# Four ordering edits in a four-layer linear-attention and gated-FFN kernel: products on zeros ahead of the work, the first K chunks slab by slab, a 16-bit exponential, and the FFN norm two steps later

## Chip, cores and metric

One core of a Trainium2 chip. The metric is the device time of one launch in microseconds (us).

## What is computed

`x` has 2048 rows of 1024 bf16 values. Layers A and B are applied in turn, twice, with the same weights:

```
x = x + A(layernorm(x));  x = x + B(layernorm(x));  x = x + A(layernorm(x));  x = x + B(layernorm(x))

A:  q, k, v = split(x @ wqkv) in 32 heads of 32;  phi(t) = (t+1 if t > 0 else exp(t)) + 1e-6
    kv = sum_s phi(k) v;  z = sum_s phi(k);  o = phi(q) kv / (phi(q) z + 1e-6);  out = o @ wo
B:  out = ((x @ w_gate) * (x @ w_up)) @ w_down          (1024 -> 3584 -> 1024)
```

## The kernel before

Rows lie in 16 tiles of 128 (`t`), four of which make a group of 512. The residual `X` stays in SBUF as bf16. Nothing is scheduled by a compiler: the program is the order in which the Python code emits instructions. Each engine takes its own in that order. Plans (`at(step, function, ...)`) say after which step of a loop a side job is emitted. Buffers come from first-in first-out lists: 16 `slots` of 1 MB, 13 `temps` of 128x512 f32, and 8 PSUM `banks`.

**Start.** SyncE (SP) issues the loads in a written order: X tiles 0 and 1, the first 512 columns of the K weights (a "slab", 1 MB, `load_cols`, L96), X tiles 2 and 3, the second K slab, X tile 4, the first V slab, and so on. Tiles 0 to 3 are normalised first. `ln_stats` (L158, L159) makes mean and variance on VectorE (DVE). `ln_norm` makes 1/sqrt on ScalarE (ACT; L166 is Ln, L168 is Exp) and the normalised tile `xn` on DVE (L170). For the first group of the first layer, `tr_tile` transposes `xn` by eight TensorE (PE) products with the identity (L187) into one bank, and ACT copies the bank to SBUF (L188). For all other groups the transpose is a DMA issued by SP (L182).

**Layer A, first loop.** A K or V chunk `kv_chunk(t, n)` is eight accumulating products of 128x128 by 128x512 (L369) of tile t with slab n (0 and 1 are K, 2 and 3 are V). It waits for its transposed tile and its slab. A group takes 16 chunks: first K for its four tiles, with slabs 0 and 1 alternating, then V. Each K chunk goes through `phi`: ACT takes exp of the bank into a temp (L193), DVE makes min(.,1)+1e-6 in the temp (L194), and DVE adds max(bank,0) to it (L195). The bank goes back only after L195. `kp` (L386) accumulates phi(k) times V. In the first layer weight statistics are taken beside it (squares on ACT L202, statistics on DVE L207).

**Layer A, second loop.** Step i of 44 emits: `den_step(i-4)` (a product L501; Ln and Exp on ACT, L503 and L506; a multiply on DVE, L509, which makes one of the eight pieces of a group's scaled phi(q)), `q_step(i)` (eight products L487, then `phi`), `out_step(i-12)` (eight products L517, one for each piece; DVE adds the bank to X, L519), then side jobs. The first `out_step` of a group, at steps 12, 20, 28 and 36, needs the eighth piece, whose L509 is emitted one step earlier. Side jobs of the first layer are maxima over weights on DVE (L222) and the weight scales. `ahead_of` plans the FFN's preparation in both A layers: for u = 0..7 statistics, norm and transpose of tile u at steps 18+2u, 19+2u and 20+2u; casts and sums of the first weights (`W.cast`, `W.sums`, L312 and L327); sums of the transposed rows (`t_sums`, L349 to L357) at steps 36 to 39.

**Layer B.** `ffn_pass` runs 14 `quad` steps of 56 products (L646) for each half of the rows, in a seven-product scheme for blocks of 2x2, and `down_seven` the way back (L868). The first quad reads the transposed rows, then `t_sums` 0, 1, 2 and 3 in that order. In the first B layer GpSimd (POOL) also casts `w_down` (`prep_load`, `prep_cast`, L571).

Of the kernel before, what the change touches and what calls it, by code (L numbers as in the profile page):

```python
# [9 lines left out]
ACT = mybir.ActivationFunctionType  # L10
ALU = mybir.AluOpType
AX = mybir.AxisListType
BF16 = mybir.dt.bfloat16
F16 = mybir.dt.float16
F32 = mybir.dt.float32
# [19 lines left out]
def kernel(  # L35
# [11 lines left out]
    nc = tc.nc  # L47
    P = 128
# [3 lines left out]
    KD = D // P  # L52
    KH = KD // 2
    KF = F // P
    G = 512
    NG = S // G
    TPG = G // P
    NB = 512
    DC = D // NB
# [7 lines left out]
    small = ctx.enter_context(tc.tile_pool(name="small", bufs=4))  # L67
# [6 lines left out]
    wqkv_v = A_wqkv.rearrange("(k p) n -> p k n", p=P)  # L74
# [7 lines left out]
    temps = Free([const.tile([P, NB], F32, tag=f"f{i}", name=f"f{i}") for i in range(13)])  # L82
    banks = Free([psum.tile([P, NB], F32, tag=f"b{i}", name=f"b{i}") for i in range(8)])

    def v3(s, n):
        return s[:].rearrange("p (k n) -> p k n", n=n)
# [4 lines left out]
    def load_x(t):  # L91
        nc.sync.dma_start(out=X[:, t, :], in_=x_view[:, t, :])

    def load_cols(view, n):
        s = slots.get()
        nc.sync.dma_start(out=v3(s, NB), in_=view[:, :, n * NB:(n + 1) * NB])  # L96
        return s

    nc.scalar.preload_act_table_set("natural_log_exp_and_others")
    wA = {}  # L100
    load_x(0)
    load_x(1)
    wA["k"] = [load_cols(wqkv_v, DC)]
    load_x(2)
    load_x(3)
    wA["k"].append(load_cols(wqkv_v, DC + 1))
    load_x(4)
    wA["v"] = [load_cols(wqkv_v, 2 * DC)]
    load_x(5)
    load_x(6)  # L110
    wA["v"].append(load_cols(wqkv_v, 2 * DC + 1))
    for t in range(7, NT):
        load_x(t)

    ident = const.tile([P, P], BF16, tag="ident", name="ident")
    make_identity(nc, ident[:])
    mask = const.tile([P, P], F32, tag="mask", name="mask")
# [30 lines left out]
    NST = D // FMAX  # L148
# [2 lines left out]
    xqs = {}  # L151
    lns = {}

    def ln_stats(li, t):
        mv = small.tile([P, 2], F32, tag="mv", name="mv")
        st = small.tile([P, NST, 6], F32, tag="st", name="st")
        for c in range(NST):
            nc.vector.bn_stats(out=st[:, c, :], in_=X[:, t, c * FMAX:(c + 1) * FMAX])  # L158
        nc.vector.bn_aggr(out=mv[:], in_=st[:])  # L159
        lns[(li, t)] = mv  # L160

    def ln_norm(li, t):
        mv = lns[(li, t)]
        half = li % 2 == 1
        rstd = small.tile([P, 1], F32, tag="rstd", name="rstd")
        nc.scalar.activation(out=rstd[:], in_=mv[:, 1:2], func=ACT.Ln, bias=(eps5x if half else eps5)[:],  # L166
                             scale=1.0 / (XS * XS) if half else 1.0)
        nc.scalar.activation(out=rstd[:], in_=rstd[:], func=ACT.Exp, scale=-0.5)  # L168
        xn = xnp.tile([P, D], F16 if half else BF16, tag="xn", name="xn")
        nc.vector.tensor_scalar(out=xn[:], in0=X[:, t, :], scalar1=mv[:, 0:1], scalar2=rstd[:],  # L170
                                op0=ALU.subtract, op1=ALU.mult)
        lns[(li, t)] = xn

    def tr_tile(li, t):
        xn = lns.pop((li, t))
        g, tl = divmod(t, TPG)
        if (li, g) not in xnTs:
            xnTs[(li, g)] = slots.get()
        s = xnTs[(li, g)]
        xnT = (h3 if li % 2 == 1 else v3)(s, NB)  # L180
        if (li, g) != (0, 0):
            nc.sync.dma_start_transpose(out=xnT[:, :, tl * P:(tl + 1) * P], in_=xn[:])  # L182
            return
        b = banks.get()
        pt = b[:].bitcast(BF16).rearrange("p (k n) -> p k n", n=P)
        for k in range(KD):
            nc.tensor.transpose(out=pt[:, k, :], in_=xn[:, k * P:(k + 1) * P], identity=ident[:])  # L187
        nc.scalar.copy(out=xnT[:, :, tl * P:(tl + 1) * P], in_=pt)  # L188
        banks.put(b)

    def phi(b, dst):
        m = temps.get()
        nc.scalar.activation(out=m[:], in_=b[:], func=ACT.Exp)  # L193
        nc.vector.tensor_scalar(out=m[:], in0=m[:], scalar1=1.0, scalar2=1e-6, op0=ALU.min, op1=ALU.add)  # L194
        nc.vector.scalar_tensor_tensor(out=dst, in0=b[:], scalar=0.0, in1=m[:], op0=ALU.max, op1=ALU.add)  # L195
        temps.put(m)

    def scan(i):
# [160 lines left out]
    def layer_A(li, ahead):  # L359
# [3 lines left out]
        def kv_chunk(t, n):  # L363
            g, tl = divmod(t, TPG)
            xnT = v3(xnTs[(li, g)], NB)
            w = v3(wA["k"][n] if n < DC else wA["v"][n - DC], NB)
            b = banks.get()
            for k in range(KD):
                nc.tensor.matmul(out=b[:], lhsT=xnT[:, k, tl * P:(tl + 1) * P], rhs=w[:, k, :],  # L369
                                 start=(k == 0), stop=(k == KD - 1))  # L370
            if n < DC:
                if g not in pks:
                    pks[g] = slots.get()
                phi(b, v3(pks[g], D)[:, tl, n * NB:(n + 1) * NB])
            else:
                c0 = (n - DC) * (NB // P)
                nc.scalar.copy(out=vbs[t % NV][:, c0:c0 + NB // P, 0:P],
                               in_=b[:].rearrange("p (c f) -> p c f", f=P))
            banks.put(b)
# [15 lines left out]
        def at(step, f, *args):  # L395
            plan.setdefault(step, []).append((f, args))

        NCH = 2 * DC * TPG
        for t in range(TPG, NT):
            i = (t // TPG - 1) * NCH + 3 * (t % TPG)  # L400
            at(i + 3, ln_stats, li, t)
            at(i + 5, ln_norm, li, t)
            at(i + 6, tr_tile, li, t)
        for t in range(NT - TPG):
            at((t // TPG + 1) * NCH + 3, kp, t)
        if li == 0:
            for t, i in ((1, 0), (2, 1), (3, 3)):
                at(i, tr_tile, li, t)
        at(2 * NCH + 4, lambda: wA.update(q=[load_cols(wqkv_v, n) for n in range(DC)]))
        at(3 * NCH + 4, lambda: wA.update(o=[load_cols(wo_v, n) for n in range(DC)]))  # L410
        if li == 0:
# [12 lines left out]
            for i, t0, t1 in ((10, 16, 24), (0, 16, 25), (1, 16, 28), (2, 20, 31), (3, 32, 36), (11, 32, 39),  # L424
# [3 lines left out]
                at(t1, spend, i, 0)  # L428
                at(t1 + 1, spend, i, 1)
        for i in range(NG * NCH):  # L430
            q, j = divmod(i, NCH)
            half, j = divmod(j, DC * TPG)
            tl, n = divmod(j, DC)
            kv_chunk(q * TPG + tl, half * DC + n)
            for f, args in plan.get(i, []):
                f(*args)
        slots.put(*wA.pop("k"), *wA.pop("v"))
# [43 lines left out]
        def q_step(g, c):  # L481
            xnT = v3(xnTs[(li, g)], NB)
            w = v3(wA["q"][c // (NB // P)], NB)
            j = c % (NB // P)
            b = banks.get()
            for k in range(KD):
                nc.tensor.matmul(out=b[:], lhsT=w[:, k, j * P:(j + 1) * P], rhs=xnT[:, k, :],  # L487
                                 start=(k == 0), stop=(k == KD - 1))
            pq[(g, c)] = temps.get()
            phi(b, pq[(g, c)][:].bitcast(BF16)[:, 0:G])  # L490
            banks.put(b)
            if c == KD - 1:
                slots.put(xnTs.pop((li, g)))
                if g == NG - 1:
                    slots.put(*wA.pop("q"))
# [279 lines left out]
    def down_seven(q, li, p, hs, wd, load_piece, cast_piece, ORDER, at, run, finish, xrow, nl, W2, load_a, final):  # L775
# [31 lines left out]
        if nl[0] < 4:  # L807
            for u in range(2 * TPG if p == 0 else TPG):
                t = nl[1] * 2 * TPG + u
                at(2 + 7 * u, ln_stats, nl[0], t)  # L810
                at(4 + 7 * u, ln_norm, nl[0], t)
                at(5 + 7 * u, tr_tile, nl[0], t)
# [81 lines left out]
    def ahead_of(li, W):  # L894
        plan = {}

        def at(step, *what):
            plan.setdefault(step, []).append(what)

        for u in range(2 * TPG):  # L900
            at(18 + 2 * u, ln_stats, li, u)
            at(19 + 2 * u, ln_norm, li, u)
            at(20 + 2 * u, tr_tile, li, u)
        at(22, W.load, 0)
        at(28, W.load, 1)
        for i in range(4):
            at(25 + i, W.cast, 0, i)
            at(34 + i, W.cast, 1, i)
            at(36 + i, t_sums, li, 0, i)
        at(35, W.sums, 0)  # L910
        at(41, W.sums, 1)
        if li == 1:
            at(36, prep_load, 0)
            at(38, prep_load, 1)
            at(40, prep_cast, 0)
        return plan

    for t in range(TPG):
        ln_stats(0, t)
        ln_norm(0, t)  # L920
        if t == 0:
            tr_tile(0, 0)
    for li in (0, 2):
        W = Weights(li)
        layer_A(li, ahead_of(li + 1, W))
        layer_B(li + 1, W)
# [30 lines left out]
```

## Time and profile before

| what | us |
|---|---|
| median of 3 runs | 1515.45 (1515.42 to 1516.24) |
| the profiled execution's own time | 1515.59 |
| span in the profile | 1513.8 |
| outside the span | 1.79 |
| PE busy | 1499.7 |
| DVE busy | 952.5 |
| ACT busy | 736.2 |
| POOL busy | 90.0 |

Times in the views count from the start of the span. A timeline row is: start, length, engine, line, operation, output and input tiles, number of merged instructions, and in brackets the engine's idle time before it with what ended it. Ends of products are modelled, so one row of products can overlap the next; starts are the sharper measure. DMA rows are issues on SP ("SPq"); the view of issues gives the time from the issue to the landing.

### The profile page before, as it was taken

How to read it: one execution, taken by the hardware profiler on the slowest of the kernel's cores; microseconds unless marked ns; L12 is line 12 of the kernel's file. 1: busy time of each engine (PE TensorE's matmuls, PEld its weight loads, DVE VectorE, ACT ScalarE, POOL GpSimd, SP SyncE). 2: the span in 40 equal slices, each digit the busy share in tenths (PEclk: the TensorE clock that was granted, in tenths of full speed). 3: DMA queues.
4: the chain of work that ended last, by engine and by line, in shares of the span. 5: the costliest groups of instructions: out<-in, count | busy, mean ns of one | idle time of the engine just before them, and what ended most of it. 6: DMA issues, size and time to landing. Idle time of an engine off the chain costs nothing.

```text
span 1513.8 us, 18314 instructions
## 1 busy us (share of the span) xinstructions
PE 1499.7 (99%) x7155; PEld 689.1 (46%) x7155; DVE 952.5 (63%) x1595; ACT 736.2 (49%) x1111; POOL 90.0 (6%) x46
## 2 busy tenths in 40 slices
PE   7999999999999999999999999999999999999999
PEld 3454444444444444444445444444444444444444
DVE  6567998988677566667355467854444853444452
ACT  4677875777535477762133365523334222333420
POOL 0000004963000000000000000000000000000000
PEclk9999999999999999999999999999999999999999
DMA  7696246475358788758413300563333678333523
GB/s 239 152 302 225 84 90 189 121 218 159 117 135 240 239 264 263 243 197 247 160 28 84 84 1 8 148 234 139 140 111 129 165 258 342 113 139 139 193 75 129
DMA packets 213399, 247.61 MB, mean 164 GB/s; under 512 B 68416, under 2 KB 189248, under 8 KB 202560
## 3 DMA queue, kind: packets, MB, share of 16 engines
q1 hardware_dynamic: 213312, 246.44, 51.6%
q8 instruction: 56, 0.92, 0.2%
q14 instruction: 31, 0.25, 0.0%
HBM read 189.79 MB, written 40.89 MB: 152 GB/s over the span
## 4 chain that ended last, share of the span: by engine, by line
PE 94%; DVE 4%; ACT 1%; DMA 1%; issue 0%; SPq 0%
PE b L646 45%; PE b L868 22%; PE b L369 12%; PE b L517 6%; PE b L487 6%; PE b L386 1%; DVE dmx L222 1%; PE b L501 1%; ACT s L202 1%; DVE wst L207 1%; DVE f L195 1%; DMA s<-in_A_wqkv_dram 1%; DVE f L194 1%; ACT f L193 0%; DVE s L195 0%; PE b L469 0%
## 5 line engine op out<-in xcount | busy, mean ns | idle before, releaser
L646 PE MATMUL b<-s,s 128*128 128x512 f16 x3136 | 677.5, 379 | 0.0
L646 PEld LDWEIGHTS <-s 128*128 128x128 f16 x3136 | 306.9, 98 | 370.0
L868 PE MATMUL b<-s,s 128*128 128x512 f16 x1568 | 339.1, 379 | 0.0
L662 DVE TENSOR_TENSOR f<-f,b 128x512 f32<-128x512 f32 x232 | 159.0, 686 | 229.1 <-ACT f L651 214.6
L651 ACT COPY f<-b 128x512 f32<-128x512 f32 x284 | 165.9, 584 | 228.0 <-PE b L646 228.0
L868 PEld LDWEIGHTS <-s 128*128 128x128 f16 x1568 | 153.4, 98 | 185.0
L369 PE MATMUL b<-s,s 128*128 128x512 bf16 x1024 | 225.0, 381 | 2.5 <-DMA s<-in_A_wqkv_dram 2.2
L369 PEld LDWEIGHTS <-s 128*128 128x128 bf16 x1024 | 100.3, 98 | 122.7 <-issue 3.9
L193 ACT ACTIVATE f<-b 128x512 f32<-128x512 f32 x128 | 75.5, 595 | 106.5 <-PE b L369 85.7
L613 ACT ACTIVATE s<-s,scw 128x1792 f16<-128x1792 bf16 x48 | 83.1, 1785 | 90.7 <-DMA s<-in_B_w_down_dram 52.7
L312 ACT ACTIVATE s<-s,scw 128x1024 f16<-128x1024 bf16 x112 | 122.9, 1152 | 3.3 <-DMA s<-in_B_w_gate_dram 2.1
L657 ACT COPY b<-b 128x512 f32<-128x512 f32 x104 | 59.2, 570 | 128.3 <-PE b L646 128.3
L517 PE MATMUL b<-s,s 128*128 128x512 bf16 x512 | 118.5, 379 | 1.9 <-DVE s L509 1.9
L487 PE MATMUL b<-s,s 128*128 128x512 bf16 x512 | 120.3, 379 | 0.0
L571 POOL TENSOR_SCALAR s<-s,scw 128x1024 f16<-128x1024 bf16 x28 | 88.3, 3170 | 263.4 <-DVE X L519 246.1
L194 DVE TENSOR_SCALAR f<-f 128x512 f32<-128x512 f32 x128 | 53.9, 421 | 75.2 <-ACT f L193 74.3
L665 DVE SCALAR_TENSOR_TENSOR s<-f,b 128x512 f16<-128x512 f32 x108 | 74.1, 686 | 40.9 <-PE b L646 24.5
L665 DVE SCALAR_TENSOR_TENSOR s<-f,f 128x512 f16<-128x512 f32 x116 | 82.5, 711 | 4.0
L158 DVE BATCH_NORM_STATS2 st<-X 128x6 f32<-128x512 bf16 x128 | 81.8, 680 | 4.4 <-DMA X<-in_A_x_dram 4.4
L517 PEld LDWEIGHTS <-s 128*128 128x128 bf16 x512 | 50.1, 98 | 62.6 <-DVE s L509 2.4
L487 PEld LDWEIGHTS <-s 128*128 128x128 bf16 x512 | 50.0, 98 | 59.6
L841 DVE SCALAR_TENSOR_TENSOR X<-b,kap,f 128x512 bf16<-128x512 f32 x48 | 32.7, 744 | 60.6 <-PE b L868 60.6
(80 smaller groups left out, 850.6 us busy)
## 6 DMA issues: line engine op xcount, KB each, us to landing
s<-wc SPq DMA_DIRECT2D x56, 1024.0 KB, 6.2
s<-dc SPq DMA_DIRECT2D x32, 896.0 KB, 6.3
wc<-s SPq DMA_DIRECT2D x28, 1024.0 KB, 4.9
s<-in_B_w_down_dram SPq DMA_DIRECT2D x24, 896.0 KB, 5.1
s<-in_B_w_down_dram SPq DMA_DIRECT2D x14, 1024.0 KB, 7.4
s<-in_B_w_gate_dram SPq DMA_DIRECT2D x28, 512.0 KB, 5.8
s<-in_B_w_up_dram SPq DMA_DIRECT2D x28, 512.0 KB, 6.8
s<-in_A_wqkv_dram SPq DMA_DIRECT2D x12, 1024.0 KB, 8.9
```

Source lines behind the costliest of these rows:

```text
L158: nc.vector.bn_stats(out=st[:, c, :], in_=X[:, t, c * FMAX:(c + 1) * FMAX])
L312: nc.scalar.activation(out=h, in_=v, func=ACT.Copy, scale=scw[:, m:m + 1])
L369: nc.tensor.matmul(out=b[:], lhsT=xnT[:, k, tl * P:(tl + 1) * P], rhs=w[:, k, :], start=(k == 0), stop=(k == KD - 1))
L487: nc.tensor.matmul(out=b[:], lhsT=w[:, k, j * P:(j + 1) * P], rhs=xnT[:, k, :], start=(k == 0), stop=(k == KD - 1))
L517: nc.tensor.matmul(out=b[:], lhsT=v3(pqs[g], G)[:, c, tl * P:(tl + 1) * P], rhs=v3(M[n], NB)[:, c, :], start=(c == 0), stop=(c == KD - 1))
L571: nc.gpsimd.tensor_scalar(out=h3(s, D)[:, i, :], in0=v3(s, D)[:, i, :], scalar1=scw[:, 2:3], scalar2=None, op0=ALU.mult)
L613: nc.scalar.activation(out=v.bitcast(F16)[:, r * w:(r + 1) * w], in_=v[:, r * w:(r + 1) * w], func=ACT.Copy, scale=scw[:, 2:3])
L646: nc.tensor.matmul(out=o[m][:], lhsT=W.get(j, m, st[i - 1], k), rhs=mv[i - 1][:, k, :], start=start and k == 0, stop=stop and k == KH - 1, ...
L651: nc.scalar.copy(out=d[m][:], in_=o[m][:])
L662: nc.vector.tensor_tensor(out=d[m][:], in0=d[m][:], in1=o[m][:], op=ALU.add)
L665: nc.vector.scalar_tensor_tensor(out=hv[:, 2 * (j % 2) + r, g * G:(g + 1) * G], in0=x[:], scalar=HS, in1=y[:], op0=ALU.mult, op1=ALU.mult)
L868: nc.tensor.matmul(out=bank[(key, tl)][:], lhsT=lhs(i, j, tl), rhs=h3(wd[2 * pi + j // WPC], NB)[:, j % WPC, :], start=(j == 0 and i in (1 ...
```

## The change

- One new helper, `warm_up(n)`, emits n products of 128x128 by 128x512 on a temp set to zero by DVE. Eleven are emitted ahead of everything else on PE, and four between tile 0's transposes and the first chunk.
- The first K slab is loaded by two DMAs of 512 KB (four of its eight row blocks each).
- The first four chunks run in the order (tile 0, slab 0), (1, 0), (0, 1), (1, 1) instead of (0, 0), (0, 1), (1, 0), (1, 1). The transposes of tiles 1, 2 and 3 are emitted inside chunks: tile 1's after the sixth product of the first chunk, tile 2's after the fourth of the third, tile 3's after the fourth of the fourth. `ln_norm` of tiles 2 and 3 and half of tile 3's statistics move into the chunks too.
- The copy out of a transpose's bank becomes two, four blocks each, and ACT's copies of tiles 0 and 1 stand ahead of the Ln and Exp of the next tile.
- `phi` writes its exponential as bf16 into the temp's first half, and both DVE instructions read it there.
- In both A layers, `ln_stats`, `ln_norm` and `tr_tile` of the FFN move from steps 18, 19, 20 + 2u to 20, 21, 22 + 2u, and `t_sums` from 36 to 39 to steps 39 to 42.

```diff
-    def load_cols(view, n):
+    def load_cols(view, n, parts=1):
         s = slots.get()
-        nc.sync.dma_start(out=v3(s, NB), in_=view[:, :, n * NB:(n + 1) * NB])
+        w = KD // parts
+        for r in range(parts):
+            nc.sync.dma_start(out=v3(s, NB)[:, r * w:(r + 1) * w, :],
+                              in_=view[:, r * w:(r + 1) * w, n * NB:(n + 1) * NB])
...
-    wA["k"] = [load_cols(wqkv_v, DC)]
+    wA["k"] = [load_cols(wqkv_v, DC, 2)]
...
+    warm = temps.get()
+    nc.vector.memset(warm[:], 0.0)
+    warmb = banks.get()
+
+    def warm_up(n):
+        for _ in range(n):
+            nc.tensor.matmul(out=warmb[:], lhsT=warm[:].bitcast(BF16)[:, 0:P], rhs=warm[:].bitcast(BF16)[:, 0:NB],
+                             start=True, stop=True)
+
+    warm_up(11)
...
-        nc.scalar.copy(out=xnT[:, :, tl * P:(tl + 1) * P], in_=pt)
+        nc.scalar.copy(out=xnT[:, 0:KH, tl * P:(tl + 1) * P], in_=pt[:, 0:KH])
+        nc.scalar.copy(out=xnT[:, KH:KD, tl * P:(tl + 1) * P], in_=pt[:, KH:KD])
...
-        nc.scalar.activation(out=m[:], in_=b[:], func=ACT.Exp)
-        nc.vector.tensor_scalar(out=m[:], in0=m[:], scalar1=1.0, scalar2=1e-6, op0=ALU.min, op1=ALU.add)
-        nc.vector.scalar_tensor_tensor(out=dst, in0=b[:], scalar=0.0, in1=m[:], op0=ALU.max, op1=ALU.add)
+        e = m[:].bitcast(BF16)[:, 0:NB]
+        nc.scalar.activation(out=e, in_=b[:], func=ACT.Exp)
+        nc.vector.tensor_scalar(out=e, in0=e, scalar1=1.0, scalar2=1e-6, op0=ALU.min, op1=ALU.add)
+        nc.vector.scalar_tensor_tensor(out=dst, in0=b[:], scalar=0.0, in1=e, op0=ALU.max, op1=ALU.add)
...
             for k in range(KD):
                 nc.tensor.matmul(out=b[:], lhsT=xnT[:, k, tl * P:(tl + 1) * P], rhs=w[:, k, :],
                                  start=(k == 0), stop=(k == KD - 1))
+                for f, *args in mid.get((t, n, k), ()):
+                    f(*args)
...
         if li == 0:
-            for t, i in ((1, 0), (2, 1), (3, 3)):
-                at(i, tr_tile, li, t)
+            order[0:4] = [(0, 0), (1, 0), (0, 1), (1, 1)]
+            mid.update({(0, 0, 5): ((tr_tile, 0, 1), (ln_norm, 0, 2), (ln_stats, 0, 3, (1,))),
+                        (1, 0, 5): ((ln_norm, 0, 3),),
+                        (0, 1, 3): ((tr_tile, 0, 2),), (1, 1, 3): ((tr_tile, 0, 3),)})
...
         for u in range(2 * TPG):
-            at(18 + 2 * u, ln_stats, li, u)
-            at(19 + 2 * u, ln_norm, li, u)
-            at(20 + 2 * u, tr_tile, li, u)
+            at(20 + 2 * u, ln_stats, li, u)
+            at(21 + 2 * u, ln_norm, li, u)
+            at(22 + 2 * u, tr_tile, li, u)
...
-            at(36 + i, t_sums, li, 0, i)
+            at(39 + i, t_sums, li, 0, i)
...
-    for t in range(TPG):
-        ln_stats(0, t)
-        ln_norm(0, t)
-        if t == 0:
-            tr_tile(0, 0)
+    ln_stats(0, 0)
+    ln_stats(0, 1, (0,))
+    ln_norm(0, 0)
+    tr_tile(0, 0)
+    ln_stats(0, 1, (1,))
+    ln_norm(0, 1)
+    ln_stats(0, 2)
+    ln_stats(0, 3, (0,))
+    warm_up(4)
+    temps.put(warm)
+    banks.put(warmb)
```

## The prediction

> **What bounds the kernel now.** First the page's busy row and its costliest groups, then the waits of PE, then the timelines of PE and DVE where those waits stand.
>
> ```profile
> PE 1499.7 (99%) x7155; PEld 689.1 (46%) x7155; DVE 952.5 (63%) x1595; ACT 736.2 (49%) x1111; POOL 90.0 (6%) x46
> ...
> L194 DVE TENSOR_SCALAR f<-f 128x512 f32<-128x512 f32 x128 | 53.9, 421 | 75.2 <-ACT f L193 74.3
> ```
>
> PE is busy 1499.7 of 1513.8 us: only PE's idle time and slow products can be won, and work on other engines counts only where PE waits for it. The second row is phi's middle instruction on DVE, 421 ns. The waits of PE, with the total, the count and the longest in us:
>
> ```profile
> PE b L187 <- DVE xn L170: 6.4, 1, 6.4
> PE b L369 <- DMA s<-in_A_wqkv_dram: 2.2, 1, 2.2
> PE b L517 <- DVE s L509: 1.9, 1, 1.9
> PE b L369 <- DVE s L195: 0.2, 1, 0.2
> ```
>
> Four waits in the whole run; the change touches all. Now the start of PE's timeline:
>
> ```profile
> 6.36 1.04 PE L187 MATMUL b<-ident,xn 128*128 128x128 bf16 x8 [6.36 <-DVE xn L170]
> 9.62 3.57 PE L369 MATMUL b<-s,s 128*128 128x512 bf16 x8 [2.22 <-DMA s<-in_A_wqkv_dram]
> 12.98 1.06 PE L187 MATMUL b<-ident,xn 128*128 128x128 bf16 x8
> 14.04 2.29 PE L369 MATMUL b<-s,s 128*128 128x512 bf16 x8
> 16.17 0.61 PE L187 MATMUL b<-ident,xn 128*128 128x128 bf16 x8
> 16.62 3.62 PE L369 MATMUL b<-s,s 128*128 128x512 bf16 x16
> 20.07 0.61 PE L187 MATMUL b<-ident,xn 128*128 128x128 bf16 x8
> 20.52 0.81 PE L369 MATMUL b<-s,s 128*128 128x512 bf16 x3
> ```
>
> Read starts against counts. The eight products from 9.62 take 3.36 us to the next row, 427 ns each after the first; from 16.62 sixteen take 3.45, 216 ns each. The weight loads, 0.43 us apart up to 14.85 and then five in 0.99 us, date the change of clock to 14.9. (The granted-clock column prints 1.00 for these stretches too, so spacing is the only sign.) Work from 9.62 to 20.52 is 32 products and 24 transposes, at full speed 32 x 0.216 + 24 x 0.056 = 8.26 us, and took 10.90.
>
> The two K slabs' rows in the view of issues (KB, us to landing):
>
> ```profile
> s<-in_A_wqkv_dram SPq DMA_DIRECT2D x1, 1024.0 KB, 7.9
> ```
> ```profile
> s<-in_A_wqkv_dram SPq DMA_DIRECT2D x1, 1024.0 KB, 10.7
> ```
>
> Issued at 1.64 and 3.31, they land at 9.6 and 14.0. The first product starts at 9.62; the first one on slab 1 at 14.04, 0.2 us after the transposes before it would let it. So the start is bound by two landings, not by the clock alone. X tile 1, next ahead of slab 0, landed at 4.1.
>
> The one long wait behind the start, on PE and then on DVE:
>
> ```profile
> 189.82 1.67 PE L517 MATMUL b<-s,s 128*128 128x512 bf16 x7
> 193.42 0.39 PE L517 MATMUL b<-s,s 128*128 128x512 bf16 x1 [1.93 <-DVE s L509]
> ```
>
> ```profile
> 187.37 2.28 DVE L222 TENSOR_REDUCE dmx<-s 128x1 f32<-128x2048 bf16 x1
> 191.55 1.28 DVE L158 BATCH_NORM_STATS2 st<-X 128x6 f32<-128x512 bf16 x2
> 192.86 0.21 DVE L159 BATCH_NORM_AGGREGATE mv<-st 128x2 f32<-128x12 f32 x1
> 192.99 0.37 DVE L509 TENSOR_TENSOR s<-f,f 128x512 bf16<-128x512 bf16 x1
> ```
>
> PE could have started its eighth product at 189.82 + 7 x 0.216 = 191.33 and started it at 193.42: 2.09 us. It lacked the L509 at 192.99, and DVE was doing the statistics of u=0 (191.55 to 192.99, 1.44 us) ahead of it, with no gap since L194 at 161.2.
>
> **Start, term by term.** The memset on DVE is bounded by the nearest rows: 0.20 us (POOL's MEMSET of 128x128 f32) and 0.69 (the slowest DVE row of 128x512 f32). DVE is idle until 3.56, so it costs nothing; PE begins at 1.0 to 1.5. Eleven products at 427 ns take 4.7 us and end by 6.2, before `xn` 0 at 6.36, so they delay nothing. The extra statistics of tile 1 (half of the 1.28 us row) fill the 0.66 us in which DVE waited for ACT before L170. Transposes 6.36 to 6.8 (at 56 ns) or 7.2 (at 107, as before).
>
> When does the clock rise? Before, 5.3 us after the first product at 9.62. The same 5.3 from 1.5 gives 6.8. [...]
>
> The four further products end at 7.7 (or 8.9 with a cold clock). ACT's copy was 1.01 us for 1024 columns; a half is about the 0.59 us of the 128x512 bank cast (L377), so the first half is in SBUF at 7.6 and the second at 8.1. Half a slab should land at 4.1 + 5.5/2 = 6.8, the other at 9.6. So four products run from 7.7, the fifth waits for 9.6, then two products, eight transposes and two products: 9.6 + 4 x 0.216 + 0.45 = 10.9. Tile 1's halves are copied by 11.4 and 12.0, so chunk (1, 0) runs from 11.4 to 13.2. Then PE waits for slab 1 at 14.0. Behind it stand 16 products and 16 transposes: 3.46 + 0.90 = 4.36, to 18.4. Before, the same four chunks and transposes ended at 20.52. **Gain 2.1 us**: 1.7 for a whole chunk moved ahead of the landing, 0.4 for the clock.
>
> This hangs on slab 1's landing. SP issues one DMA more ahead of it (0.43 us), but the bytes ahead are the same, so I take 14.0. Bounds: one X tile's spacing in landings, 0.7 us (10.3 to 11.0 for tiles 2 and 3), either way, so 1.4 to 2.8. The chain ahead has 0.8 us of slack, so a late second half of slab 0 or a late clock costs nothing up to there. The norm of tiles 2 and 3 moves behind tile 1's transposes; with X landing at 10.3 and 11.0 it is on DVE by 13.1 and 14.5, and needed at 14.9 and 17.0. The two half copies cost ACT 0.17 us more per tile, beside PE's products.
>
> **phi in 16 bits.** ACT writes as many elements (595 ns against 586 for the cast to bf16): nothing. L195 reads PSUM, like L519, which with a bf16 operand takes 682 against 692: nothing. For L194 the nearest rows are 421 (itself, f32) and 276 (L450, 128 columns); L170 takes 544 for 1024 bf16 columns, half of it 272. I take 290, near the low end, because L170 is the nearest in kind (one bf16 input, bf16 out) and halving it halves its fixed part too, which is too low: 0.13 us saved each. [...] 128 of them save DVE 17 us, and PE nothing but at two places. At 119.4 PE waited 0.39 us (48 products from 109.06 end at 119.43, the next starts at 119.82) for a bank that L195 frees; six L194 lie ahead of it since 108.6, 0.8 us. **Gain 0.39** (bounds 0 and 0.39).
>
> **FFN norm two steps later.** At 191.33 the L509 that PE needs is preceded by 1.44 us less (statistics now behind the group's last piece) and by seven quicker L194, 0.93. It starts at 190.6 and ends at 191.0, ahead of 191.33. With L194 unchanged it would end at 191.9, and 0.6 us would stay. **Gain 2.05** (bounds 1.44 and 2.09). What is late next: DVE's steps 20 to 27 carry 2.0 us of norm every two steps beside 1.9 a step, 5.8 against PE's 7.3, so it catches up before the next group's first product at step 28. On ACT, Ln stands two steps later, so the Ln that blocked ACT for 4.3 us (188.8 to 193.1) now waits less.
>
> At the tail everything is later. Tile 7's statistics come at step 34 and its norm at 35, so SP issues its transpose near 245.5 instead of 241.2, and behind it on SP stand the `w_down` loads and quad 2's weights, 4.3 us later each. POOL's casts start at 253, not 248.6, and end their first block at 266 against DVE's use at 273. On DVE `t_sums` 0 ends near 250.6, 1 at 252.3, 2 at 254.3, `W.sums` at 256.8, `t_sums` 3 at 258.6. FFN reads them at 257.4, 258.2, 260.0 and 263.4: hidden, by 4.8 us at the tightest. In layer 2 DVE has gaps, no weight sums, and PE no wait: nothing won or lost.
>
> **Sum.** 2.1 + 0.39 + 2.05 = 4.6 us. The profiled execution took 1515.59 (1.79 outside the span, unchanged), 0.14 above the median, inside the spread: 1511.0. Best ends: 2.8 + 0.39 + 2.09 = 5.3, 1510.3; worst: 1.4 + 0 + 1.44 = 2.8, 1512.8.
>
> **Rivals.** (a) Products on zeros do not raise the clock. For it: no row shows such products. Against: before, the clock rose after products alone. Then, cold, the first chunk runs from 8.9 to 13.2 (eight products and eight transposes, 4.3 us), chunk (1, 0) half cold to 14.9 and half warm to 15.8, and the 4.36 behind it end at 20.1: the start gains 0.4, all three 2.8, 1512.8. (b) Slab 1 lands 1.5 us late because the split disturbs the queue (slab 0 took 5.5 us, slab 1 3.0 from the landing before it, so the first is not at the queue's full rate). The start gains 0.6: 1512.6. (c) On the slow side: tile 7's transpose and the sums, three steps later, reach the first quad late. It decides when DVE or SP lag 4.8 us more than I sum; if `t_sums` 3 came 13 us late (four POOL casts of 3.2 us, should DVE queue behind them), PE would wait 8.2 and the time be 1515.6 - 4.6 + 8.2 = 1519.2. Against: DVE has no such wait there before.
>
> **Chances.** Mine 0.72, (a) 0.12, (b) 0.08, (c) 0.08. A measurement can tell about 0.2%, 3.0 us: (a) and (b) fall inside it, (c) outside on the slow side. The range takes the best end, and (a) and (b) with some of their terms at the worst: 1510.0 to 1513.6.
>
> **What would show it.** PE's second row of products starts near 7.7, at 216 ns; a wait for `in_A_wqkv` near 13.2 to 14.0; the fifth chunk (tile 2) starts near 18.4; no row L517 <- L509, and no L369 <- L195; L194 near 290 ns; the first quad 4.6 us earlier than 255.64. Wrong if products are 427 ns apart behind 9, if slab 1 lands behind 14.7, or if L646 waits for a DVE or DMA row.

## The result, and the profile after

The changed kernel took 1511.19 us in the median of seven runs (1510.23 to 1511.85), beside 1515.45 us of the kernel before in seven runs (1514.43 to 1517.05). The ratio is 0.997 with a 95% interval of 0.9958 to 0.9981. The profiled execution is the slowest of the seven: 1511.85 us with a span of 1509.8, against 1515.59 and 1513.8 before, 4.0 us less span.

The waits of PE in the kernel after (total, count, longest, in us). The lines of the code have moved: L369 is now L386, L517 is L538, L509 is L530, L194 is L211, L195 is L212, L646 is L667, L158 and L159 are L172 and L175; the products on zeros are L124.

```profile
PE b L386 <- DMA s<-in_A_wqkv_dram: 1.6, 3, 0.8
PE b L124 <- DVE f L119: 1.4, 1, 1.4
PE b L538 <- DVE s L530: 0.3, 1, 0.3
PE b L386 <- ACT s L203: 0.2, 1, 0.2
```

The long wait for `xn` (6.4 us) is filled with zeros and no longer a wait, and the wait of 0.2 us for L212 is gone. The row L538 <- L530, which was to go, is still there; it is shorter, and it stands elsewhere. PE's timeline at the start (a few records of products are missing from the trace: x3 at 14.12 stands for four):

```profile
1.44 4.88 PE L124 MATMUL b<-f 128*128 128x512 bf16 x11 [1.44 <-DVE f L119]
6.43 0.62 PE L202 MATMUL b<-ident,xn 128*128 128x128 bf16 x8
6.89 1.03 PE L124 MATMUL b<-f 128*128 128x512 bf16 x4
8.29 1.02 PE L386 MATMUL b<-s,s 128*128 128x512 bf16 x4 [0.38 <-DMA s<-in_A_wqkv_dram]
9.74 0.59 PE L386 MATMUL b<-s,s 128*128 128x512 bf16 x2 [0.43 <-DMA s<-in_A_wqkv_dram]
...
11.46 1.90 PE L386 MATMUL b<-s,s 128*128 128x512 bf16 x8 [0.25 <-ACT s L203]
14.12 1.02 PE L386 MATMUL b<-s,s 128*128 128x512 bf16 x3 [0.77 <-DMA s<-in_A_wqkv_dram]
...
17.61 4.70 PE L386 MATMUL b<-s,s 128*128 128x512 bf16 x21
```

The first eleven products start 427 ns apart; the eight transposes from 6.43 take 0.46 us to the next row, 56 ns each, so the clock rose between 5.68 and 6.43. The trace's record of the granted clock (the share of full speed that PE is given) dates the rise to 6.22. (This record begins with the first rise, at 14.90 in the kernel before; the column prints 1.00 ahead of it, as the prediction noted, but it does show later falls.) Everything behind runs at 216 ns. PE is through with both chunks of slab 0 at 13.2, waits for slab 1 (landed at 14.08), and starts the fifth chunk four products behind 17.61, at 18.47 instead of 20.52.

The middle instruction of phi on the page of after, and then the new place of the L530 wait, on PE and on DVE:

```profile
L211 DVE TENSOR_SCALAR f<-f 128x512 bf16<-128x512 bf16 x128 | 36.9, 288 | 81.0 <-ACT f L210 80.4
```
```profile
239.25 1.04 PE L538 MATMUL b<-s,s 128*128 128x512 bf16 x4 [0.29 <-DVE s L530]
```
```profile
237.38 1.28 DVE L172 BATCH_NORM_STATS2 st<-X 128x6 f32<-128x512 bf16 x2
238.69 0.21 DVE L175 BATCH_NORM_AGGREGATE mv<-st 128x2 f32<-128x12 f32 x1
238.82 0.37 DVE L530 TENSOR_TENSOR s<-f,f 128x512 bf16<-128x512 bf16 x1
```

L211 takes 288 ns (421 before). At the old place of the L530 wait (189.82 to 193.42 before) PE goes on without a gap:

```profile
187.37 1.89 PE L538 MATMUL b<-s,s 128*128 128x512 bf16 x7
189.10 0.38 PE L522 MATMUL b<-f,s 128*128 128x512 bf16 x1
```

Its eight products (one record is missing) take 1.73 us to the next row, 8 x 0.216. But at 239.25 the first product of step 36, the first of group 3's output, waits for the eighth piece of its hidden tile, and on DVE that L530 stands behind the statistics of u=7, which the change moved from step 32 to step 34. From start to start PE loses 0.46 us there (0.67 instead of 0.216). It is the wait of 191.33 over again, at another boundary.

All kernels can be laid beside each other by three times of their profiled executions: when slab 1 landed; how far behind it the first product of the K and V sums starts (L386 before, L405 after: the end of the start phase); and how far behind that the first quad starts (everything between). Behind the first quad nothing differs: the last product of all starts 1254.4 to 1254.5 us later in each.

| kernel | slab 0, slab 1 landed | slab 1 to first K and V sum | from there to first quad | first quad | median of runs |
|---|---|---|---|---|---|
| before | 9.57, 14.00 | 34.15 | 207.49 | 255.64 | 1515.45 |
| after | 9.70, 14.08 | 32.01 | 205.47 | 251.56 | 1511.19 |
| z_only | 9.78, 14.19 | 35.41 | 207.51 | 257.11 | 1516.51 |
| z_fill | 10.28, 14.62 | 34.77 | 207.51 | 256.90 | 1515.87 |
| no_zeros | 7.94, 12.29 | 33.81 | 205.46 | 251.56 | 1511.93 |
| no_split | 8.88, 13.25 | 32.01 | 205.46 | 250.72 | 1510.94 (one) |
| norm_back | 8.93, 13.34 | 32.01 | 206.31 | 251.66 | 1512.06 |
| f32_exp | 8.55, 12.92 | 32.01 | 206.66 | 251.59 | 1511.99 |
| u7_late | 8.95, 13.32 | 32.01 | 205.00 | 250.33 | 1510.67 |
| x3_late | 8.71, 12.38 | 32.01 | 205.48 | 249.87 | 1509.93 |
| best | 8.58, 12.30 | 32.01 | 205.01 | 249.32 | 1509.62 |
| best_no_zeros | 8.04, 11.72 | 34.67 | 205.00 | 251.39 | 1511.33 |
| best_no_split | 10.46, 14.15 | 34.15 | 205.00 | 253.30 | 1512.19 |
| after_again | 8.94, 13.27 | 32.01 | 205.47 | 250.75 | 1510.86 |

The columns come apart cleanly. The third is a property of the start's order and clock, the fourth one of phi and the FFN, to 0.02 us; what differs between the two profiled runs of the kernel after is the landing. The kernel no_split was timed once only. The kernel before, run beside the experiments, had medians of 1515.01 (with z_only, no_zeros, no_split, norm_back), 1515.42 (f32_exp, u7_late, x3_late, best) and 1515.69 us (the others).

### The profile page after: what moved, and what is told of

Its sections match the earlier page's. It is cut to its first block, busy times and chain, and to the rows that moved or that the text cites. A ratio compares the mean times of both kernels' runs of the same rounds, so it can differ in the third digit from the quotient of the medians.

```text
span 1509.8 us, 18303 instructions
## 1 busy us (share of the span) xinstructions
PE 1500.2 (99%) x7122; PEld 689.6 (46%) x7170; DVE 940.1 (62%) x1596; ACT 737.0 (49%) x1115; POOL 90.3 (6%) x46
## 4 chain that ended last, share of the span: by engine, by line
PE 98%; DVE 1%; DMA 1%; issue 0%; SPq 0%; DVEq 0%
PE b L667 45%; PE b L889 22%; PE b L386 14%; PE b L508 7%; PE b L538 7%; PE b L405 1%; PE b L522 1%; DMA s<-in_A_wqkv_dram 1%; PE b L490 0%; DVE st L172 0%; DVE X L540 0%; SPq L92 0%; DVE s L530 0%; DVE xn L185 0%; SPq L98 0%
## 5 line engine op out<-in xcount | busy, mean ns | idle before, releaser
L667 PE MATMUL b<-s,s 128*128 128x512 f16 x3136 | 677.5, 379 | 0.0
L667 PEld LDWEIGHTS <-s 128*128 128x128 f16 x3136 | 306.8, 98 | 370.0
L386 PE MATMUL b<-s,s 128*128 128x512 bf16 x1000 | 221.5, 379 | 3.1 <-DMA s<-in_A_wqkv_dram 1.6
L386 PEld LDWEIGHTS <-s 128*128 128x128 bf16 x1024 | 99.7, 98 | 121.3 <-issue 2.2
L210 ACT ACTIVATE f<-b 128x512 bf16<-128x512 f32 x128 | 75.6, 596 | 105.9 <-PE b L386 83.5
L508 PE MATMUL b<-s,s 128*128 128x512 bf16 x504 | 119.5, 379 | 0.3
L538 PE MATMUL b<-s,s 128*128 128x512 bf16 x496 | 117.7, 379 | 1.1 <-DVE s L530 0.3
L211 DVE TENSOR_SCALAR f<-f 128x512 bf16<-128x512 bf16 x128 | 36.9, 288 | 81.0 <-ACT f L210 80.4
L172 DVE BATCH_NORM_STATS2 st<-X 128x6 f32<-128x512 bf16 x128 | 81.9, 680 | 3.5 <-DMA X<-in_A_x_dram 3.5
L538 PEld LDWEIGHTS <-s 128*128 128x128 bf16 x512 | 50.0, 98 | 61.0 <-DVE s L530 1.0
```

The source lines that it names most:

```text
L538: nc.tensor.matmul(out=b[:], lhsT=v3(pqs[g], G)[:, c, tl * P:(tl + 1) * P], rhs=v3(M[n], NB)[:, c, :], start=(c == 0), stop=(c == KD - 1))
L667: nc.tensor.matmul(out=o[m][:], lhsT=W.get(j, m, st[i - 1], k), rhs=mv[i - 1][:, k, :], start=start and k == 0, stop=stop and k == KH - 1, ...
```

## Experiments: the start

**z_only**, the zeros alone:

```diff
 # kernel before
+    warm_up(11)
...
             tr_tile(0, 0)
+            warm_up(4)
```

> The kernel before, with nothing but the products on zeros (eleven ahead of everything, four behind tile 0's transposes). My theory, that two landings bind the start: the first chunk still waits for all of slab 0 (9.6 us) and now runs at 216 ns, the third chunk still waits for slab 1 (14.0), so the fifth chunk starts near 20.1 instead of 20.52, a gain of 0.4 us in the whole run. Rival, that the slow clock is the whole of the start's loss: the first 32 products and 24 transposes take 8.3 us from 9.6, the fifth chunk starts at 17.9, a gain of 2.6 us.

Both are wrong. The fifth chunk starts at 21.97, 1.45 us later than before (1.26 at an equal landing of slab 1, 35.41 against 34.15 in the table), and the time is 1516.51 against 1515.01 us (ratio 1.001, interval 1.000 to 1.002). PE's timeline shows why:

```profile
11.55 0.61 PE L197 MATMUL b<-ident,xn 128*128 128x128 bf16 x8
14.23 2.34 PE L379 MATMUL b<-s,s 128*128 128x512 bf16 x8 [2.07 <-DMA s<-in_A_wqkv_dram]
16.36 1.06 PE L197 MATMUL b<-ident,xn 128*128 128x128 bf16 x8
17.21 4.47 PE L379 MATMUL b<-s,s 128*128 128x512 bf16 x16
```

The first chunk is fast now, and so PE is idle from 12.0 to 14.23, until slab 1 is there. The eight products behind take 2.13 us instead of 1.73, and the transposes from 16.36 take 0.85 us, 107 ns each: the clock has fallen again. The record of the granted clock has it rise at 5.28, fall to 0.50 at 15.52 and rise at 18.94. Here the clock that the zeros had bought was lost again behind the wait for a landing that PE had reached 2.2 us early. Why this idle stretch and not the one before it was not shown: PE was also idle for 2.1 us from 7.68 to 9.82, and the clock stayed up until 15.52.

**z_fill**, with eight more zeros in that idle stretch:

```diff
 # z_only
+    def fill():
+        warm_up(8)
+        temps.put(warm)
+        banks.put(warmb)
...
             for t, i in ((1, 0), (2, 1), (3, 3)):
                 at(i, tr_tile, li, t)
+            at(0, fill)
```

> The kernel with only the products on zeros, and eight more of them behind tile 1's transposes, where PE stood idle from 12.0 to 14.2 us and the clock fell 1.5 us later. My theory now, that the idle stretch makes the clock fall: products and transposes stay at 216 and 56 ns from 6.4 on, and the fifth chunk starts 6.1 us behind slab 1's landing (24 products and 16 transposes), near 20.2; against 7.8 us with only the zeros and 6.5 before, so 1.7 us faster than the one and 0.4 faster than before. Rival, that zeros raise the clock only for a set time, whatever follows: it falls again near 15.5 and the kernel stays slower than before.

```profile
10.32 3.36 PE L384 MATMUL b<-s,s 128*128 128x512 bf16 x8 [2.40 <-DMA s<-in_A_wqkv_dram]
...
13.96 1.89 PE L121 MATMUL b<-f 128*128 128x512 bf16 x8
15.69 1.89 PE L384 MATMUL b<-s,s 128*128 128x512 bf16 x7
```

The number is missed (fifth chunk at 21.76, median 1515.87), and the run does not test the theory. Slab 0 landed only at 10.28, and PE was idle from 7.76 on, a stretch that holds no zeros; the clock fell at 9.92, and the first chunk ran at 427 ns. It rose again at 13.34, ahead of the eight further zeros. The stretch that these fill was only 0.7 us long here, from 13.96 to slab 1's landing at 14.62, and they ran on until 15.69: they held PE up for 1.07 us. From there the fifth chunk comes 6.07 us later, as expected; without the 1.07 the distance from slab 1's landing to the first K and V sum would be 33.7 instead of 34.77, 0.4 to 0.5 below the 34.15 of before (an estimate from these numbers, not run). The rival, a set time after which the clock falls, is refuted by the kernel after instead: its clock rose at 6.22 and fell only at 1511.49, behind the last product.

**no_zeros**, the other way round:

```diff
 # kernel after
-    warm_up(11)
...
-    warm_up(4)
```

> The kernel after, without its fifteen products on zeros. My theory: products and transposes from 6.4 on run at 427 and 107 ns until the clock rises some 5 us after the first dense products, near 13 to 15 us; chunk (1, 0) then ends near 15 instead of 13.2 and takes the slack ahead of slab 1, and the fifth chunk starts near 19.3 to 20.0 instead of 18.47: 0.8 to 1.5 us of the start's 2.05 are lost. Rival, that the landing alone binds and the zeros do nothing: the fifth chunk stays at 18.5.

```profile
8.12 2.74 PE L385 MATMUL b<-s,s 128*128 128x512 bf16 x6 [0.68 <-ACT s L202]
10.65 1.06 PE L201 MATMUL b<-ident,xn 128*128 128x128 bf16 x8
11.50 3.65 PE L385 MATMUL b<-s,s 128*128 128x512 bf16 x14
14.99 0.61 PE L201 MATMUL b<-ident,xn 128*128 128x128 bf16 x8
```

The fifth chunk starts at 18.47 again, as the rival has it, but not because zeros do nothing. Slab 1 landed 1.8 us earlier in this run, and PE didn't wait for it: on the slow clock until 11.99, it began chunk (1, 0) at 12.39 and reached slab 1 four products ahead of 14.99, at 14.13, as late as the landing in the profiled run of after. So what zeros are worth is about 14.13 less the landing: nothing in that run, 1.8 us in this one. (About, because the rise moves from run to run: in best_no_zeros, below, a clock that rose at 13.02 made it 14.42.) Over ten runs the median is 1511.93, against 1511.19 and 1510.86 with zeros: 0.7 to 1.1 us.

**no_split**, slab 0 in one DMA:

```diff
 # kernel after
-    wA["k"] = [load_cols(wqkv_v, DC, 2)]
+    wA["k"] = [load_cols(wqkv_v, DC)]
```

> The kernel after, with slab 0 of the K weights in one DMA again. My theory: the first product moves from 8.29 to the landing of the whole slab near 9.6, chunk (0, 0) ends near 11.9 and chunk (1, 0) near 13.9, still ahead of slab 1 at 14.1, so the fifth chunk stays within 0.2 us of 18.47 and the whole within 0.2 us. Rival, that the split carries a part of the gain: the fifth chunk comes 1.3 us later, as much as the first product does.

The first product starts at 8.92, and the distance from slab 1's landing to the first K and V sum is 32.01 as with the split: no loss, as my theory has it, but with nothing to spare: PE was through with slab 0 at 13.24, and slab 1 landed at 13.25. (The fifth chunk is at 17.63, outside the 0.2 us, since slab 1 landed 0.83 us earlier.)

**x3_late**, X tile 3 behind slab 1:

```diff
 # kernel after
     load_x(2)
-    load_x(3)
     wA["k"].append(load_cols(wqkv_v, DC + 1))
+    load_x(3)
...
-            mid.update({(0, 0, 5): ((tr_tile, 0, 1), (ln_norm, 0, 2), (ln_stats, 0, 3, (1,))),
-                        (1, 0, 5): ((ln_norm, 0, 3),),
-                        (0, 1, 3): ((tr_tile, 0, 2),), (1, 1, 3): ((tr_tile, 0, 3),)})
+            mid.update({(0, 0, 5): ((tr_tile, 0, 1), (ln_norm, 0, 2)),
+                        (0, 1, 5): ((ln_stats, 0, 3),), (1, 1, 5): ((ln_norm, 0, 3),),
+                        (0, 1, 3): ((tr_tile, 0, 2),), (2, 0, 5): ((tr_tile, 0, 3),)})
...
-    ln_stats(0, 3, (0,))
```

> The kernel after, with X tile 3's load issued behind slab 1 instead of ahead of it, and its statistics, norm and transposes later in the first chunks. My theory, that slab 1 binds by the bytes ahead of it: it lands 0.7 us earlier (13.4 instead of 14.1) and the fifth chunk starts near 17.8 instead of 18.47. Rival, that the queue's order does not set slab 1's landing or that tile 3 becomes late: the fifth chunk stays at 18.5 or comes later.

Slab 1 lands 3.67 us behind slab 0 instead of 4.38, 0.71 less, which is one X tile; in the table the distance is 4.33 to 4.43 in all ten kernels with the old order and 3.67 to 3.72 in the four with the new one. The distance behind the landing stays at 32.01, and the median is 1509.93. The first K and V sum starts 1.70 us earlier than in after; 1.0 of this is slab 0's earlier landing in this run, 0.7 the edit. (The fifth chunk itself starts 2.15 us earlier, at 16.32, four and eight products of 0.216 us behind a row at 13.73, since tile 3's transposes, 0.45 us, now stand behind its start.)

## Experiments: phi and the FFN

**norm_back**:

```diff
 # kernel after
-            at(20 + 2 * u, ln_stats, li, u)
-            at(21 + 2 * u, ln_norm, li, u)
-            at(22 + 2 * u, tr_tile, li, u)
+            at(18 + 2 * u, ln_stats, li, u)
+            at(19 + 2 * u, ln_norm, li, u)
+            at(20 + 2 * u, tr_tile, li, u)
...
-            at(39 + i, t_sums, li, 0, i)
+            at(36 + i, t_sums, li, 0, i)
```

> The kernel after, with the FFN norm and the sums of w_down at their old steps. My theory: PE's wait for L530 near 190 comes back with 1.44 us of statistics ahead of it, less 0.93 for seven quicker L211, so about 1.2 us (2.09 less 0.93); the wait of 0.46 us before the first product of step 36, which the statistics of u=7 cause, goes. Net about 0.7 us slower than the kernel after at the first quad. Rival, that the wait near 190 hung on the f32 exp alone: it stays away, and the kernel is 0.46 us faster than the kernel after.

```profile
189.44 0.39 PE L538 MATMUL b<-s,s 128*128 128x512 bf16 x1 [1.13 <-DVE s L530]
```

The wait is back at the group's eighth product, 1.30 us from start to start, and PE has no gap near step 36. Net 206.31 against 205.47, 0.84 us slower (0.7 expected); the median is 1512.06.

**f32_exp**:

```diff
 # kernel after
-        e = m[:].bitcast(BF16)[:, 0:NB]
+        e = m[:]
```

> The kernel after, with exp's output in f32 again. My theory: L211 takes 421 ns again, the wait of PE for a bank near 119 comes back with 0.39 us, PE waits about 0.6 us for L530 near 190, and the wait before step 36 stays at 0.46 or grows: 1.0 us or more slower than the kernel after at the first quad, and nothing more behind it. Rival, that DVE's time only fills its own gaps: the 17 us that L211 then takes more cost nothing but the 0.39.

Its waits of PE:

```profile
PE b L538 <- DVE s L530: 0.9, 2, 0.6
...
PE b L386 <- DVE s L212: 0.2, 1, 0.2
```

L211 takes 421 ns again. From start to start PE loses 0.40 us for the bank at 116, 0.71 at 187.9 and 0.52 at 238.5: 1.63 against 0.46 in after, so 1.17 us, and the table's fourth column says 1.19. The rival's 0.39 is too small: of 17 us on DVE, 1.2 reach PE, at the places where DVE is late at a boundary (0.40, 0.71 and, over what after has there, 0.06), and PE does not feel the rest.

**u7_late**, a test of the new wait:

```diff
 # kernel after
-            at(20 + 2 * u, ln_stats, li, u)
-            at(21 + 2 * u, ln_norm, li, u)
-            at(22 + 2 * u, tr_tile, li, u)
+            d = 20 + 2 * u + u // 7
+            at(d, ln_stats, li, u)
+            at(d + 1, ln_norm, li, u)
+            at(d + 2, tr_tile, li, u)
```

> The kernel after, with the statistics, the norm and the transpose of the last tile of the layer (u=7) one step later, at 35, 36 and 37. My theory: the statistics of u=7 then stand behind the eighth piece of group 3, which PE needs for the first product of step 36; PE's wait of 0.46 us before that product goes, and the first quad starts 0.47 us earlier (251.1 instead of 251.56). Rival, that DVE is late there by its own total: the eighth piece stays late, the wait moves by a few products and keeps its size.

```profile
237.08 0.43 DVE L530 TENSOR_TENSOR s<-f,f 128x512 bf16<-128x512 bf16 x1 [0.37 <-ACT f L527]
237.42 0.68 DVE L540 TENSOR_TENSOR X<-X,b 128x512 bf16<-128x512 bf16 x1
238.02 1.28 DVE L172 BATCH_NORM_STATS2 st<-X 128x6 f32<-128x512 bf16 x2
```

The eighth piece now stands ahead of the statistics, DVE even waits for ACT before it, and the row L538 <- L530 is gone. The way to the first quad is 205.00, 0.47 us shorter, as expected. DVE was late by its order there, not by its total.

## Experiments: both edits together, and what zeros and split are worth then

**best** is x3_late and u7_late together:

```diff
 # kernel after
+    (the edits of x3_late)
+    (the edits of u7_late)
```

> The kernel after with both: X tile 3's load behind slab 1, and the last tile's norm one step later. Both theories: 0.7 and 0.47 us, about 1.15 us faster than the kernel after at the first quad, and as much in the end. If only one of them holds, its part alone.

Its waits of PE:

```profile
PE b L124 <- DVE f L119: 1.4, 1, 1.4
PE b L202 <- DVE xn L185: 0.4, 1, 0.4
PE b L386 <- ACT s L203: 0.2, 1, 0.2
```

No row of a wait for a DMA is left, nor one behind 11 us; by the starts, 0.2 us of idle time remain ahead of slab 1's first product at 12.35. The two columns give what was expected, 0.66 us (slab 1 lands 3.72 behind slab 0 instead of 4.38) and 0.46; the rest of the 2.24 us at the first quad is slab 0's earlier landing. The median is 1509.62 us (1509.46 to 1510.03), the ratio to before 0.9963 (0.9951 to 0.9976). That is 1.2 to 1.6 us below the two medians of after; the 13 runs of after lie between 1510.23 and 1511.85, none as low as the highest of these five.

**best_no_zeros**:

```diff
 # best
-    warm_up(11)
...
-    warm_up(4)
```

> The kernel with both further edits (X tile 3 behind slab 1, the last tile's norm later), without its products on zeros. My theory: PE, on the slow clock until 12.4, reaches slab 1's first product at 14.1 whatever the landing, which is near 12.3 here; the first quad starts 1.8 us later than with the zeros (251.1 instead of 249.3). Rival, that the zeros are worth no more than 0.7 us, the difference of the medians without and with them in the kernel after.

The first quad is at 251.39, 2.1 us later than with zeros although slab 1 landed 0.6 us earlier, and the median is 1511.33, 1.7 us more. The clock rose at 13.02 here (11.99 in no_zeros), and PE reached slab 1 at 14.42, which is the 0.3 us over my number. With an early landing the zeros are worth 1.7 us in the medians, against 0.7 to 1.1 in after.

**best_no_split**:

```diff
 # best
-    wA["k"] = [load_cols(wqkv_v, DC, 2)]
+    wA["k"] = [load_cols(wqkv_v, DC)]
```

> The kernel with both further edits, with slab 0 of the K weights in one DMA again. My theory: with slab 1 landing near 12.3 the split begins to count: the first product comes with the whole slab at 8.6 to 8.9 instead of 7.6, chunk (1, 0) ends 0.9 to 1.1 us later, near 13.2, and the fifth chunk, and the first quad, are 0.8 to 0.9 us later than with the split (250.2 instead of 249.3). Rival: no difference, as in the kernel after, where slab 1 landed at 13.25.

```profile
10.50 2.72 PE L386 MATMUL b<-s,s 128*128 128x512 bf16 x6 [2.43 <-DMA s<-in_A_wqkv_dram]
```

The direction is right, the size is not: the first quad is 4.0 us later. Slab 0 landed at 10.46 in this run, PE was idle from 7.9 to 10.5, and the clock fell (10.19 to 13.60 by its record), so six products take 2.52 us to the next row (13.02) and the third column is 34.15. The eight timed runs spread from 1510.56 to 1513.42, those of best over 0.6 us. So the split was worth nothing in the kernel after, where the whole slab landed at 8.88, and 2.14 us (34.15 less 32.01) beside the late landing itself here. Of these, 0.66 need no slow clock: at full speed PE is through with slab 0 4.35 us after its landing (8.88 to 13.24 in no_split), and slab 1 lands only 3.69 behind it here. The other 1.48 go with the clock (an estimate from these rows). That the clock would have stayed up with the split in this very run is argued from after, where slab 0's halves landed 1.45 us apart, PE worked in between and the clock did not fall; it wasn't run at such a landing.

**after_again** is the kernel after, unchanged.

> The kernel after once more, for its spread beside these. My theory, that its start hangs on slab 1's landing alone, which the profiled runs of kernels with the same DMAs in the same order have between 12.3 and 14.1: the first product of K and V sums stands 32.01 us behind that landing again, whatever the landing is, the waits behind are the same, and the median of the times is 1510.5 to 1511.5. Rival: the distance varies with the landing.

Slab 1 landed at 13.27 and the two distances are 32.01 and 205.47, as in the first profile, with a landing 0.81 us earlier. The median is 1510.86 us (ratio 0.9969, 0.9957 to 0.9981). The profiled run of after thus had the latest slab 1 of the seven kernels that order these DMAs alike (12.29 to 14.08).

## Why the prediction was right, and where it wasn't

**The sum.** It said 4.6 us and 1511.0 (its terms as written, 2.1 + 0.39 + 2.05, make 4.54); the medians say 4.3 (and 4.8 in after_again's comparison), the two profiled runs 4.08 at the first quad. In these, 4.08 = 2.06 (start) + 0.39 + 2.09 (the FFN wait) - 0.46 (the new wait). At an equal landing of slab 1 it would be 4.16, 2.14 and 2.02 in the two columns. That the medians come as near to 4.6 as they do is in part luck: a wait that was not foreseen takes 0.46 us, and landings of slab 1 earlier than the 14.0 assumed (13.27 in after_again) give some of it back. The 1.79 us outside the span, taken as unchanged, were 2.02 in the profiled run of after, and 1.77 to 2.15 over all kernels. The time alone could hardly tell the rivals (1512.8 and 1512.6) from the sum; the traces do, and none of them came in.

**Start: the sum right, two of its terms not.** The fifth chunk was put at 18.4 and came at 18.47; the gain of 2.1 was 2.06. The step "a half slab should land at 6.8" failed: the half landed at 8.25, so first products started at 8.29, not 7.7. It put the second half 2.8 us behind the first; eight of the nine traces with the split have 1.36 to 1.61 (x3_late 2.48), and the first half at 6.23 to 8.25. The slack ahead of slab 1 took this, as the text said it would. The other term is "1.7 for a whole chunk moved ahead of the landing, 0.4 for the clock": with slab 1 at 14.08, no_zeros says that the rest of the start's edits gives all but 0.05 us of it, since a PE without zeros reaches slab 1 at 14.13; and z_only shows that zeros alone lose 1.26 at an equal landing rather than gain 0.4. The terms don't add; they are a maximum of two times. Zeros pay here since the clock stays up behind them (with the reordering PE is idle for 0.9 us at most in after, by the starts, and the clock did not fall; z_only has 2.2 and it did), and only as far as slab 1 lands ahead of the 14.1 to 14.4 that PE needs without them. "I take 14.0" for slab 1, with 0.7 us either way, was the latest case rather than the middle one: seven kernels after the change had it between 12.29 and 14.08. The three kernels without the reordering had it between 14.00 and 14.62; whether the change itself brings it forward is open. The half copies on ACT were not run apart.

**Rival (a)**, that zeros don't raise the clock, is refuted by the 56 ns transposes at 6.43. It priced a clock that stays low and my own term one that stays high; neither priced one that rises and falls again. In z_only it rose at 5.28, fell at 15.52 and rose again at 18.94. Transposes start 56 ns apart with the clock up (from 6.43 in after) and 107 with it down (from 16.36 in z_only). Whether transposes alone would raise it was not run. **Rival (b)**, that the split delays slab 1, has nothing for it: slab 1 lands 4.3 to 4.4 us behind slab 0 with and without the split.

**phi.** L194 was put at 290 ns and took 288. The wait at 119.4 went (0.39), and L212, at 692 ns, gained nothing, as said. That the 17 us on DVE are worth something "at two places" only was right but for 0.06 us at a third, step 36.

**FFN norm.** The gain at 191.33 was 2.09 (2.05 said). The step that failed is "What is late next": the text followed DVE to the first product of step 28, found it caught up, and stopped. The same boundary comes again at step 36, and there the statistics of u=7, now at step 34, stand ahead of the eighth piece: 0.46 us back. u7_late shows that this is all of it.

**Tail and rival (c).** Hidden, as summed: PE has no wait between 239.3 and the first quad, in after or in any variant, and layer 2 neither gains nor loses. The margin is smaller than the 4.8 us said: `t_sums` 3 ends at 255.6 in after, and its reader, 36 products of 0.216 us behind the first quad, stands at 259.3.

## What to carry to other kernels

When a stage ends with a load's landing, take the distance from that landing to the next fixed point as your measure; it was constant to 0.01 us in the eight kernels whose PE is ready ahead of the landing, where the times of whole runs varied by 1.6. In z_only a faster clock ahead of a late load was worth nothing and the time rose by 1.5 us: TensorE then stood idle for 2.2 us (12.0 to 14.23), and the clock fell under the work behind, at 15.52. So bring work or a load forward together with the warming. And when a block of work is moved in a repeating schedule, follow it past every boundary that it now stands before, the last one too.

## What the runs showed of the hardware

- The clock rose 2.8 to 6.0 us after the first product on zeros at 1.44 (at 4.23 in no_split, 5.28 in z_only, 6.76 in after_again, 7.42 in u7_late), in kernels whose first eleven products are the same.
- Ahead of the last product the clock fell in three of the fourteen traces: in z_only at 15.52, 1.3 us behind an idle stretch of TensorE of 2.2 us (12.0 to 14.23); in z_fill at 9.92, inside one of 2.6 us (7.76 to 10.32); in best_no_split at 10.19, inside one of 2.6 us (7.9 to 10.5). It was low for 3.4 us each time, until 18.94, 13.34 and 13.60. The idle stretch of 2.1 us in z_only (7.68 to 9.82) brought no fall. What decides between them was not shown.
- The landing of slab 0 varies from run to run: 7.94 to 9.70 in two DMAs (nine kernels), 8.88 to 10.46 in one (five kernels), 8.7 and 9.8 in the mean. Whether the split itself makes it earlier, and what sets the variation, is open; X tile 1, next ahead, landed at 4.09 to 4.27 in all of them.
- Slab 1 landed 4.33 to 4.43 us behind slab 0 in the ten kernels with X tiles 2 and 3 between them on the queue, and 3.67 to 3.72 us in the four with X tile 2 alone, 256 KB less; slab 0 itself landed between 7.94 and 10.46.
